# Router products turned before they are stored, the first segment's left q and k taken from SBUF, and one load and one store for each routed row

## The chip, the cores and the metric

The kernel runs on one core of a Trainium2 chip. The metric is the device time of one execution in microseconds (us); less is better. Engines are called as in the profile: PE (TensorE, matmuls and transposes), DVE (VectorE), ACT (ScalarE), POOL (GpSimd) and SP (SyncE). DMAs are issued from two queues here: SP's and POOL's. The core's 16 DMA engines work on both.

## What is computed

The output is `x + A(xn) + B(xn)`, where `xn` is the layer norm of `x` (2048 rows of 1024).

```python
def _A_ref(x, mem0, Wq, Wk, Wv, Wo, seg_len):      # H = 32 heads of 128, M = 8, seg_len = 32
    ...
    for s in range(n_seg):                          # 64 segments
        xs = x[:, s * seg_len:(s + 1) * seg_len, :].copy()
        h = jnp.concatenate([mem, xs], axis=1)      # 8 memory rows and 32 rows of x
        q, k, v = ...                               # h @ Wq, Wk, Wv
        scores = jnp.where(mask, q k^T * scale, -1e9)
        o = softmax(scores) v @ Wo
        mem = o[:, :M, :].copy()                    # memory for the next segment
        outs.append(o[:, M:, :])
    return jnp.concatenate(outs, axis=1)

def _B_ref(x, w_r, w_gate, w_up, w_down):
    r = x @ w_r                                     # one number for each row: the router
    idx = jnp.argsort(-r, axis=-1)[:, :2]           # the two best rows
    ...
    y = silu(x_sel @ w_gate) * (x_sel @ w_up) @ w_down
    y = y * sigmoid(r_sel)                          # added to these two rows of the output
```

## The kernel before, in words

**Segments.** A is sequential: a segment needs the memory of the one before. Of its 32 rows, 24 are computed in the chain together with the 8 memory rows of the carry (the main rows, 32 columns of a stationary operand). The last 8 rows of each segment are called left rows. They are not needed for their own memory, so those of four segments (32 rows) go through the weights together, in the shadow of the main rows. Their q and k are put to DRAM (`ql_d`) and fetched by the segment that needs them; their v stays in SBUF.

**Weights.** Wq, Wk, Wv and Wo are 64 granules of 512 KB. 43 stay in SBUF (`wres`); 21 are streamed through five slots (`g`) in every segment, one of them being kept in PSUM instead, and a quarter of another. In the first segment all granules come from the inputs, and POOL copies the streamed ones to DRAM scratch (`wsc`, line 337), from which later segments read them (line 313). A segment runs six phases of eight granules (q and k of heads 0 to 15, q and k of heads 16 to 31, v of both halves, lines 600 to 643), then the output projection WO over the 16 granules of Wo (lines 646 to 690).

**The order of work** is written out by hand. Each engine and each DMA queue works off its instructions in program order. `hooks[p, kc]` holds what PE and the others do after granule kc of phase p: the turn of a phase's q or k (line 481) at granule 3 of the next phase, scores of half 0 at (2, 6) and of half 1 at (4, 6), the softmax at (3, 0) and (5, 0). `after(s, g)` (line 411) runs behind granule g: in the first segment it also issues the router's steps (`side`), block copies, x loads and resident loads, and `fetch()` issues the next streamed granule, which must wait on SP for a free slot.

**Around the change.** While a phase has left rows, `behind` (line 608) holds their passes and `after` back until the fourth granule. The router: line statistics of all rows, then 16 calls of `router_tile` (line 209, two DVE passes over 128 x 1024 each) behind granules 18 to 33; `router_out` (line 216) behind granule 34; `router_top` (line 220) behind granule 42, which reads the 2048 products back as one row (RROW) and finds the two best with MAX8 and FIND_INDEX8. The scratch for this lies in places of resident granules that come late: XR and RROW in the place of granule 61, MISC (RF, RB) in that of 63, the x rows XP in those of 49 to 60, XP7 (the last router tiles) in that of 49. So a Wo granule can be loaded only when the tile in its place has been read (lines 420 and 421).

The first segment's left q and k go the same way as the others': evacuated as XBl (line 633), stored to `ql_d` by four DMAs (line 636), and, since no later segment fetches them, loaded again by `scores` (line 499) itself: `new_lx(0, half)` clears a tile and loads four strips of 16 rows, `turn_lx` turns it into QKL, and `left_keys` copies the left k beside the main k.

**The end.** Lines 729 to 797: the two routed rows of x are loaded, normalised and turned; two rows of the output are loaded as four halves (ROW, line 767); the gate and up weights (GU), then the down weights (YP) are multiplied; YP is copied out of PSUM (line 792), scaled and added to ROW (line 794), and stored as four halves (line 797). T0 holds x of the two rows first and the copied YP later. Source and target rows are chosen by values that POOL reads from the index tile.

Of the kernel before, what the change touches and what calls it, by code (L numbers as in the profile page):

```python
# [8 lines left out]
BF16 = mybir.dt.bfloat16  # L9
F32 = mybir.dt.float32  # L10
U32 = mybir.dt.uint32
ALU = mybir.AluOpType
# [15 lines left out]
def kernel(  # L28
# [16 lines left out]
    nc = tc.nc  # L45
    P = 128
# [8 lines left out]
    NT = S // P  # L55
# [5 lines left out]
    XL = M  # L61
# [3 lines left out]
    out2 = out[0]  # L65
# [26 lines left out]
    one = ctx.enter_context(tc.tile_pool(name="one", bufs=1, reuse_waits="tile"))  # L92
    rot = ctx.enter_context(tc.tile_pool(name="rot", bufs=3, reuse_waits="tile"))
# [10 lines left out]
    r_d = dram.tile([1, S], BF16, name="r_d")  # L104
# [3 lines left out]
    def home(g, shape, dtype, name):  # L108
        return wres.tile(shape, dtype, name=name, tag=f"wres{g}")
# [105 lines left out]

    def router_out():
        nc.vector.tensor_copy(out=RB, in_=RF)
        nc.gpsimd.dma_start(out=r_d[0].rearrange("(t p) -> p t", p=P), in_=RB)

    def router_top():  # L220
        RROW = home(hx, [1, S], BF16, "RROW")
# [207 lines left out]

    n_x_left = list(range(n_x, NT // 2))  # L430

    def new_lx(s, half=None):

        t = lx[0] = one.tile([P, 512], BF16, tag="pt", name="LX") if half is None else \
            rot.tile([P, 512], BF16, tag="xb", name="LX")
        G, j = divmod(s, 4)
        if half is None:
            nc.gpsimd.dma_start(out=t[:, :], in_=ql_d[G][j])
        else:
            nc.vector.memset(t[:, :], 0.0)  # L440
            for jq in range(4):
                nc.gpsimd.dma_start(out=t[32 * jq + 16 * half:32 * jq + 16 * half + 16, :],
                                    in_=ql_d[G][j, 32 * jq + 16 * half:32 * jq + 16 * half + 16, :])

    lx = [None]

    def turn_lx():
        PTq = PTB.rearrange("p (i c) -> p i c", i=4)
        for il in range(4):
            nc.tensor.transpose(out=PTq[:, il, :], in_=lx[0][:, il * P:(il + 1) * P], identity=IDENT[:, :])  # L450
        t = qkl[0] = one.tile([P, 16, 4, XL], BF16, tag="qkl", name="QKL")
        nc.scalar.copy(out=t.rearrange("p h c r -> p (h c r)"), in_=PTq.rearrange("p i c -> p (i c)"))  # L452

    qkl = [None]
    todo = []
# [12 lines left out]
    for s in range(NSEG):  # L468
# [12 lines left out]
        def transposes(mat, half, XB):  # L481
            PTq = PTB.rearrange("p (i j r) -> p i j r", i=4, j=4)
            for il in range(4):
                nc.tensor.transpose(out=PTq[:, il, :, :].rearrange("p j r -> p (j r)"), in_=XB[:, il * P:(il + 1) * P],  # L484
                                    identity=IDENT[:, :])
            pv = PTq.rearrange("p i j r -> p (i j) r")
            if mat == 0:
                QT[half] = one.tile([P, 16, 32], BF16, tag="qt", name="QT")
                nc.scalar.copy(out=QT[half][:, :, :], in_=pv)
            else:  # L490
                KT[half] = one.tile([P, 16, NK], BF16, tag="kt", name="KT")
                if s > 0:
                    left_keys(half)
                nc.vector.tensor_copy(out=KT[half][:, :, 0:32], in_=pv)  # L494

        def left_keys(half):
            nc.vector.tensor_copy(out=KT[half][:, :, 32:NK], in_=qkl[0][:, :, 2 * half + 1, :])  # L497

        def scores(half):
            if s == 0:  # L500
                new_lx(0, half)
                turn_lx()
                left_keys(half)
            QKL = qkl[0]
            q, k = QT[half], KT[half]
            for il in range(4):
                for jq in range(4):
                    hh = 4 * il + jq
                    nc.tensor.matmul(SPS[32 * jq:32 * jq + 32, il, 0, :], lhsT=q[:, hh, :], rhs=k[:, hh, :],
                                     start=(il == 0), stop=True, tile_position=(0, 32 * jq), skip_group_check=True)  # L510
                    nc.tensor.matmul(SPS[32 * jq:32 * jq + XL, il, 1, :], lhsT=QKL[:, hh, 2 * half, :],  # L511
                                     rhs=k[:, hh, :], start=False, stop=True, tile_position=(0, 32 * jq),
                                     skip_group_check=True)
            S4 = SPS.rearrange("p i a k -> p i (a k)")
            nc.vector.tensor_tensor(out=S4, in0=S4, in1=MASK[:, :].unsqueeze(1).to_broadcast([P, 4, 2 * NK]), op=ALU.add)  # L515
            S8 = SPS.rearrange("p i a k -> p (i a) k")
            NM = one.tile([P, 8], F32, tag="nm", name="NM")
            nc.vector.tensor_reduce(out=NM[:, :], in_=S8, axis=AX.X, op=ALU.max, negate=True)
            nc.vector.tensor_tensor(out=S8, in0=S8, in1=NM[:, :].unsqueeze(2).to_broadcast([P, 8, NK]), op=ALU.add)
# [80 lines left out]
        for p, (mat, half) in enumerate(PHASES):  # L600
            PSm = psA.tile([P, 512], F32, tag="acc", name="PSm")
            PSl, done = None, []
            if mat in left:
                PSl, done = started.pop((s, p), (None, []))
                if PSl is None:
                    PSl = psL.tile([P, 512], F32, tag="accl", name="PSl")
            rest = [8 * p + kc for kc in range(KC) if 8 * p + kc not in done]
            behind = []
            for kc in range(KC):
                g = 8 * p + kc  # L610
                Gv = granule(g)
                for jq in range(4):
                    nc.tensor.matmul(PSm[32 * jq:32 * jq + 32, :], lhsT=ST[:, kc, :], rhs=Gv[:, 512 * jq:512 * (jq + 1)],  # L613
                                     start=(kc == 0), stop=(kc == KC - 1), tile_position=(0, 32 * jq))
                if g in kept_at and s == 0:
                    keep(g, Gv)
                behind.append((g, Gv))
                if PSl is None or kc >= 3 or not left_before:
                    for g_, Gv_ in behind:
                        if PSl is not None and g_ not in done:  # L620
                            left_pass(PSl, g_, Gv_, not done and g_ == rest[0], g_ == rest[-1])
                        after(s, g_)
                    behind = []
                for fn in hooks.pop((p, kc), []):
                    fn()
            left_before = PSl is not None
            if mat < 2:
                XB = rot.tile([P, 512], BF16, tag="xb", name="XB")
                nc.scalar.copy(out=XB[:, :], in_=PSm[:, :])  # L629
                hooks.setdefault((p + 1, 3), []).insert(0, lambda m=mat, h=half, b=XB: transposes(m, h, b))  # L630
                if PSl is not None:
                    XBl = rot.tile([P, 512], BF16, tag="xb", name="XBl")
                    nc.scalar.copy(out=XBl[:, :], in_=PSl[:, :])  # L633
                    c0 = 16 * half + 8 * mat
                    for jq in range(4):
                        nc.gpsimd.dma_start(out=ql_d[left[mat]][:, 32 * jq + c0:32 * jq + c0 + 8, :],  # L636
                                            in_=XBl[32 * jq:32 * jq + 32, :])
            else:
                c0 = half * 512
                VM[half] = rot.tile([P, 512], BF16, tag="xb", name="VM")  # L640
                nc.scalar.copy(out=VM[half][:, :], in_=PSm[:, :])  # L641
                if PSl is not None:
                    nc.scalar.copy(out=VL[:, c0:c0 + 512], in_=PSl[:, :])
# [117 lines left out]
    nc.tensor.matmul(PSG[0:2, 0:1], lhsT=SIGR, rhs=ONE1, start=True, stop=True)  # L761
    SIG = T2[0:2, 52:54].bitcast(F32)
    nc.vector.tensor_copy(out=SIG, in_=PSG[0:2, 0:1])
    ROW = rot.tile([2, 512], BF16, tag="xb", name="ROW0"), rot.tile([2, 512], BF16, tag="xb", name="ROW1")
    for c in range(2):
        for a in range(2):
            nc.gpsimd.dma_start(out=ROW[a][c:c + 1, :], in_=out2[bass.ds(vals[c], 1), 512 * a:512 * (a + 1)])

    GU = psA.tile([P, 512], F32, tag="acc", name="GU")
    for w in range(2):  # L770
# [12 lines left out]
    for fg in range(FC // 2):  # L783
        Gt = moe_tiles["dn", fg]
        for a in range(2):
            fc = 2 * fg + a
            for dh in range(2):
                nc.tensor.matmul(YP[dh][0:2, :], lhsT=HT[:, fc, :], rhs=Gt[:, a * D + dh * 512:a * D + (dh + 1) * 512],
                                 start=(fc == 0), stop=(fc == FC - 1))
    YB = T0[0:2, :]  # L790
    for dh in range(2):
        nc.vector.tensor_copy(out=YB[:, 512 * dh:512 * (dh + 1)], in_=YP[dh][0:2, :])
    for a in range(2):
        nc.vector.scalar_tensor_tensor(out=ROW[a][:, :], in0=YB[:, 512 * a:512 * (a + 1)], scalar=SIG[:, 0:1],
                                       in1=ROW[a][:, :], op0=ALU.mult, op1=ALU.add)
        for c in range(2):
            nc.gpsimd.dma_start(out=out2[bass.ds(vals[c], 1), 512 * a:512 * (a + 1)], in_=ROW[a][c:c + 1, :])


# [33 lines left out]
```

## Time and profile before

| what | value |
|---|---|
| three runs | 2170.11, 2173.65 (median), 2186.66 us |
| the profiled execution | 2172.97 us, of which the span of the page is 2171.4 us |
| PE, DVE, ACT, POOL busy | 78%, 36%, 31%, 30% of the span |
| DMA moved | 754.62 MB, mean 348 GB/s |
| first store of segment 0's output | 151.6 us |
| first store of the last segment's output | 2100.5 us |
| last output store issued | 2161.96 us |

Rows of a timeline read: start, duration, engine, line, operation, tiles out<-in, shape, count, and in brackets how long the engine was idle before and who ended that. A stretch (window) gives for each engine its busy time and instructions, then the clock granted to PE (1.00 is full), the mean busy share of the DMA engines, and what they moved. A tile's view ends with the least, median and largest time from issue to landing of its DMAs.

### The profile page before, as it was taken

The numbers are of one execution on the slowest core, as the hardware profiler recorded it, in microseconds if no ns is written. First come the engines' busy times: TensorE is split into PE (matmuls) and PEld (weight loads), VectorE is DVE, ScalarE is ACT, GpSimd is POOL, SyncE is SP. The second block draws the span as 40 slices with busy tenths as digits, with TensorE's granted clock in tenths as the row PEclk, the third lists the DMA queues.
The fourth block names the chain that finished last, engine by engine and source line by source line (L and its number), as shares of the span: only waits on it lengthen the run. The fifth ranks groups of instructions, "written<-read, shape, count | busy, mean of one in ns | idle before, by whom it ended". The sixth has DMA issues, their size and how long they took to land.

```text
span 2171.4 us, 82642 instructions
## 1 busy us (share of the span) xinstructions
PE 1683.9 (78%) x36007; PEld 904.3 (42%) x36007; DVE 781.9 (36%) x2463; ACT 671.1 (31%) x1865; POOL 643.6 (30%) x1218
## 2 busy tenths in 40 slices
PE   3247787878888887888888888878888788888754
PEld 1124444444444444445444444444444444444433
DVE  5613333332333333333333333333333333334320
ACT  0013233333333333333333333333333233333320
POOL 4223233332323233323323322332323233232120
PEclk8669999999999999999999999999999999999986
DMA  9989899998999999999999999999999999999996
GB/s 363 378 248 367 327 352 344 369 355 319 366 343 372 337 355 361 348 366 340 348 336 374 349 346 365 328 337 339 376 339 355 339 341 355 328 371 358 376 384 245
DMA packets 245244, 754.62 MB, mean 348 GB/s; under 512 B 49872, under 2 KB 56176, under 8 KB 244880
## 3 DMA queue, kind: packets, MB, share of 16 engines
q1 hardware_dynamic: 203440, 712.46, 88.0%
q0 software_dynamic: 41440, 36.86, 5.8%
q8 instruction: 282, 4.62, 0.9%
q14 instruction: 82, 0.67, 0.1%
HBM read 736.39 MB, written 22.95 MB: 350 GB/s over the span
## 4 chain that ended last, share of the span: by engine, by line
DMA 52%; PE 31%; issue 7%; ACT 4%; POOL 4%; DVE 2%; SPq 0%; ACTq 0%; DVEq 0%; POOLq 0%
DMA g<-wsc 34%; PE PSm L613 11%; DMA ql_d<-XBl 9%; PE WO L661 8%; DMA XL<-in_A_x_dram 3%; PE PSl L596 3%; PE WL L661 2%; POOL ql_d L636 2%; PE BO L549 2%; DMA LX<-ql_d 1%; POOL XL L272 1%; DMA XP<-in_A_x_dram 1%; ACT VM L641 1%; PE BT L251 1%; ACT XBl L633 1%
## 5 line engine op out<-in xcount | busy, mean ns | idle before, releaser
L613 PE MATMUL PSm<-wres,ST 128*32 128x512 bf16 x8192 | 702.1, 390 | 6.3 <-DVE ST L266 5.4
L613 PEld LDWEIGHTS <-ST 128*32 128x32 bf16 x12288 | 335.5, 96 | 598.4 <-issue 311.0
L613 PE MATMUL PSm<-g,ST 128*32 128x512 bf16 x4096 | 416.5, 390 | 204.0 <-DMA g<-wsc 186.2
L629 ACT CAST XB<-PSm 128x512 bf16<-128x512 f32 x256 | 150.2, 587 | 389.4 <-PE PSm L613 387.3
L636 POOL DMA_DIRECT2D ql_d<-XBl x256 | 152.9, 604 | 378.3 <-ACT XBl L633 364.5
L661 PE MATMUL WO<-wres,OT 128*32 128x256 bf16 x5632 | 254.8, 290 | 4.2 <-issue 4.1
L238 POOL DMA_DIRECT2D X<-in_A_x_dram x256 | 132.8, 526 | 366.8 <-PE WO L647 264.8
L706 POOL DMA_DIRECT2D out_dram<-OB x256 | 128.5, 509 | 378.5 <-DVE OB L704 373.0
L661 PEld LDWEIGHTS <-OT 128*32 128x32 bf16 x8192 | 207.9, 101 | 78.2 <-issue 44.0
L596 PE MATMUL PSl<-wres,STL 128*32 128x512 bf16 x2048 | 196.2, 394 | 1.1
L661 PE MATMUL WO<-g,OT 128*32 128x256 bf16 x2560 | 139.6, 294 | 26.3 <-DMA g<-wsc 15.2
L641 ACT CAST VM<-PSm 128x512 bf16<-128x512 f32 x128 | 76.9, 601 | 267.0 <-PE PSm L613 215.0
L556 DVE CAST OT<-BT 128x128 bf16<-128x128 f32 x128 | 37.3, 292 | 303.6 <-PE BT L551 303.6
L556 ACT CAST OT<-BO 128x128 bf16<-128x128 f32 x256 | 68.1, 266 | 220.4 <-PE BT L551 219.4
L549 PE MATMUL BO<-PT,VM 32*128 32x40 bf16 x1024 | 94.3, 180 | 45.6 <-ACT VM L641 42.1
L497 DVE COPY KT<-QKL 128x128 bf16<-128x128 bf16 x128 | 24.6, 192 | 266.2 <-ACT QKL L452 266.2
L549 PEld LDWEIGHTS <-VM 32*128 32x128 bf16 x2048 | 67.2, 92 | 122.0 <-issue 56.1
L515 DVE TENSOR_TENSOR BS<-BS,MASK 128x320 f32<-128x320 f32 x128 | 63.9, 500 | 134.9 <-PE BS L511 134.9
L596 PEld LDWEIGHTS <-STL 128*32 128x32 bf16 x3072 | 85.4, 99 | 57.9 <-issue 14.1
L494 DVE COPY KT<-BT 128x512 bf16<-128x512 bf16 x128 | 54.1, 422 | 148.4 <-PE BT L484 148.0
L246 POOL TENSOR_TENSOR X<-X,XN 128x256 bf16<-128x256 bf16 x64 | 42.8, 669 | 207.4 <-DVE XN L244 207.0
L596 PE MATMUL PSl<-g,STL 128*32 128x512 bf16 x1024 | 103.8, 389 | 0.1
(148 smaller groups left out, 2364.2 us busy)
## 6 DMA issues: line engine op xcount, KB each, us to landing
g<-wsc SPq DMA_DIRECT2D x1197, 512.0 KB, 6.3
g<-wsc SPq DMA_DIRECT2D x63, 384.0 KB, 4.7
ql_d<-XBl POOLq DMA_DIRECT2D x256, 32.0 KB, 5.9
LX<-ql_d POOLq DMA_DIRECT2D x63, 128.0 KB, 5.3
MW<-in_B_w_gate_dram SPq DMA_DIRECT2D x16, 448.0 KB, 9.4
MW<-in_B_w_up_dram SPq DMA_DIRECT2D x16, 448.0 KB, 9.3
wres<-in_A_Wk_dram SPq DMA_DIRECT2D x12, 512.0 KB, 12.3
wres<-in_A_Wo_dram SPq DMA_DIRECT2D x11, 512.0 KB, 6.9
```

Source lines behind the costliest of these rows:

```text
L238: nc.gpsimd.dma_start(out=X[s % 2][32 * g:32 * g + XM, :], in_=x2[s * SEG:s * SEG + XM, 256 * g:256 * (g + 1)])
L494: nc.vector.tensor_copy(out=KT[half][:, :, 0:32], in_=pv)
L515: nc.vector.tensor_tensor(out=S4, in0=S4, in1=MASK[:, :].unsqueeze(1).to_broadcast([P, 4, 2 * NK]), op=ALU.add)
L549: nc.tensor.matmul(o, lhsT=VM[half][q0:q0 + 32, il * P:(il + 1) * P], rhs=PTm[q0:q0 + 32, il, 0:NK], start=True, stop=False, tile_position ...
L556: copy(out=OT[half][:, 2 * ph + jl, :, :], in_=ov[:, :, 0:SEG])
L596: nc.tensor.matmul(PSl[32 * jq:32 * jq + 32, :], lhsT=STL[:, g % KC, :], rhs=Gv[:, 512 * jq:512 * (jq + 1)], start=first_, stop=last_, til ...
L613: nc.tensor.matmul(PSm[32 * jq:32 * jq + 32, :], lhsT=ST[:, kc, :], rhs=Gv[:, 512 * jq:512 * (jq + 1)], start=(kc == 0), stop=(kc == KC - ...
L629: nc.scalar.copy(out=XB[:, :], in_=PSm[:, :])
L636: nc.gpsimd.dma_start(out=ql_d[left[mat]][:, 32 * jq + c0:32 * jq + c0 + 8, :], in_=XBl[32 * jq:32 * jq + 32, :])
L641: nc.scalar.copy(out=VM[half][:, :], in_=PSm[:, :])
L661: nc.tensor.matmul(PS[32 * g:32 * g + 32, 0:256], lhsT=lhs(h), rhs=Gv[:, D * hs + 256 * g:D * hs + 256 * (g + 1)], start=False, stop=(last ...
L706: nc.gpsimd.dma_start(out=out2[s * SEG:s * SEG + XM, 256 * g:256 * (g + 1)], in_=OB[32 * g:32 * g + XM, :])
```

## The change

Three edits. `router_out` has PE turn the 128 x 16 products into 16 x 128, DVE copies them from PSUM to a new tile RT (in the place of granule 61), and the store writes 16 rows of 128 numbers. For the first segment the left q or k of a phase is turned from XBl directly, by four transposes and one ACT copy that takes the columns of segment 0 into QKL, just ahead of the turn of the same phase's main rows; so `scores` loads nothing, and the left k goes beside the main k where it does in other segments. XBl is still stored to `ql_d`. At the end ROW is one tile of two rows of 1024, in T0; each row is loaded by one DMA and stored by one, and the sum reads YP from PSUM.

```diff
     def router_out():
         nc.vector.tensor_copy(out=RB, in_=RF)
-        nc.gpsimd.dma_start(out=r_d[0].rearrange("(t p) -> p t", p=P), in_=RB)
+        nc.tensor.transpose(out=PTB[0:NT, 0:P], in_=RB, identity=IDENT[:, :])
+        RT = home(hx, [NT, P], BF16, "RT")
+        nc.vector.tensor_copy(out=RT[:, :], in_=PTB[0:NT, 0:P])
+        nc.gpsimd.dma_start(out=r_d[0].rearrange("(t p) -> t p", p=P), in_=RT[:, :])
...
-    def new_lx(s, half=None):
...
+    def new_lx(s):
+        t = lx[0] = one.tile([P, 512], BF16, tag="pt", name="LX")
         G, j = divmod(s, 4)
...
+        nc.gpsimd.dma_start(out=t[:, :], in_=ql_d[G][j])
...
+    def turn_first(mat, half, XBl):
+        if mat == 0 and half == 0:
+            qkl[0] = one.tile([P, 16, 4, XL], BF16, tag="qkl", name="QKL")
+        PTq = PTB.rearrange("p (i c) -> p i c", i=4)
+        for il in range(4):
+            nc.tensor.transpose(out=PTq[:, il, :], in_=XBl[:, il * P:(il + 1) * P], identity=IDENT[:, :])
+        nc.scalar.copy(out=qkl[0][:, :, 2 * half + mat, :], in_=PTB.rearrange("p (h s r) -> p h s r", s=4, r=XL)[:, :, 0, :])
...
                 KT[half] = one.tile([P, 16, NK], BF16, tag="kt", name="KT")
-                if s > 0:
-                    left_keys(half)
+                left_keys(half)
...
         def scores(half):
-            if s == 0:
-                new_lx(0, half)
-                turn_lx()
-                left_keys(half)
...
                     c0 = 16 * half + 8 * mat
+                    if s == 0:
+                        hooks[p + 1, 3].insert(0, lambda m=mat, h=half, b=XBl: turn_first(m, h, b))
...
-    ROW = rot.tile([2, 512], BF16, tag="xb", name="ROW0"), rot.tile([2, 512], BF16, tag="xb", name="ROW1")
+    ROW = T0[0:2, :]
     for c in range(2):
-        for a in range(2):
-            nc.gpsimd.dma_start(out=ROW[a][c:c + 1, :], in_=out2[bass.ds(vals[c], 1), 512 * a:512 * (a + 1)])
+        nc.gpsimd.dma_start(out=ROW[c:c + 1, :], in_=out2[bass.ds(vals[c], 1), :])
...
-    YB = T0[0:2, :]
     for dh in range(2):
-        nc.vector.tensor_copy(out=YB[:, 512 * dh:512 * (dh + 1)], in_=YP[dh][0:2, :])
-    for a in range(2):
-        nc.vector.scalar_tensor_tensor(out=ROW[a][:, :], in0=YB[:, 512 * a:512 * (a + 1)], scalar=SIG[:, 0:1],
-                                       in1=ROW[a][:, :], op0=ALU.mult, op1=ALU.add)
-        for c in range(2):
-            nc.gpsimd.dma_start(out=out2[bass.ds(vals[c], 1), 512 * a:512 * (a + 1)], in_=ROW[a][c:c + 1, :])
+        cols = slice(512 * dh, 512 * (dh + 1))
+        nc.vector.scalar_tensor_tensor(out=ROW[:, cols], in0=YP[dh][0:2, :], scalar=SIG[:, 0:1], in1=ROW[:, cols],
+                                       op0=ALU.mult, op1=ALU.add)
+    for c in range(2):
+        nc.gpsimd.dma_start(out=out2[bass.ds(vals[c], 1), :], in_=ROW[c:c + 1, :])
```

More of the change, by code (lines that the diff above doesn't have):

```diff
@@ L430 @@
     n_x_left = list(range(n_x, NT // 2))
-    def new_lx(s, half=None):
-        t = lx[0] = one.tile([P, 512], BF16, tag="pt", name="LX") if half is None else \
-            rot.tile([P, 512], BF16, tag="xb", name="LX")
+    def new_lx(s):
+        t = lx[0] = one.tile([P, 512], BF16, tag="pt", name="LX")
         G, j = divmod(s, 4)
[L437 to L443, printed above, removed]
+        nc.gpsimd.dma_start(out=t[:, :], in_=ql_d[G][j])
     lx = [None]
```

## The prediction

> **What bounds it now.** I read the page first, then stretches of the first 150 us and the timeline there engine by engine, then the last 20 us. All three edits lie in the first segment or behind the last one.
>
> ```profile
> span 2171.4 us, 82642 instructions
> GB/s 363 378 248 367 327 352 344 369 355 319 366 343 372 337 355 361 348 366 340 348 336 374 349 346 365 328 337 339 376 339 355 339 341 355 328 371 358 376 384 245
> DMA 52%; PE 31%; issue 7%; ACT 4%; POOL 4%; DVE 2%; SPq 0%; ACTq 0%; DVEq 0%; POOLq 0%
> ```
>
> Each number of the second line is a slice of 54 us. The third slice, 109 to 163 us, moves 248 GB/s, less than any but the last, in a kernel whose chain is half DMA. The stretches below cut it finer (columns: busy of PE, PEld, DVE, ACT, POOL, then granted clock, DMA share, GB/s).
>
> ```profile
> 60.00:98.00 38.00, 10.36 (x172) 4.88 (x172) 27.88 (x58) 5.02 (x8) 10.74 (x19) 0.65 1.03 403
> 98.00:106.00 8.00, 0.00 (x0) 0.00 (x0) 3.35 (x8) 0.00 (x0) 4.72 (x8) 0.50 0.87 295
> 106.00:124.00 18.00, 0.00 (x0) 0.00 (x0) 0.00 (x0) 0.00 (x0) 0.57 (x1) 0.50 1.01 100
> 124.00:134.00 10.00, 4.52 (x82) 2.49 (x86) 2.98 (x9) 2.08 (x4) 2.66 (x5) 0.55 1.00 371
> 134.00:142.00 8.00, 6.86 (x189) 4.10 (x182) 5.92 (x9) 3.51 (x16) 3.31 (x6) 1.00 0.77 243
> 142.00:148.00 6.00, 1.15 (x24) 0.97 (x24) 0.00 (x0) 0.00 (x0) 0.00 (x0) 0.60 1.03 384
> ```
>
> Up to 98 us the first segment runs at the DMA's rate, 403 GB/s: it brings in all weights, and copies the streamed ones for the later segments. Then come 18 us at 100 GB/s with the engines "busy" (share 1.01) and all of PE, DVE and ACT idle. What was issued there, and who waited:
>
> ```profile
> 101.16 1.19 POOL L218 DMA_DIRECT2D r_d<-MISC  x1 [3.50 <-DVE MISC L217]
> 123.43 0.69 POOL L337 DMA_DIRECT2D wsc<-in_A_Wo_dram  x1 [17.55 <-DMA r_d<-MISC]
> 125.03 0.50 POOL L222 DMA_DIRECT2D RROW<-r_d  x1 [0.92 <-DMA wsc<-in_A_Wv_dram]
> ...
> DMA to landing us min/median/max: 7.3/14.7/22.0
> ...
> 73.82 0.58 PE L450 MATMUL BT<-IDENT,LX 128*128 128x128 bf16 x4 [14.68 <-DMA LX<-ql_d]
> 128.58 0.59 PE L450 MATMUL BT<-IDENT,LX 128*128 128x128 bf16 x4 [43.35 <-DMA LX<-ql_d]
> 146.85 0.62 PE L661 MATMUL WO<-g,OT 128*32 128x256 bf16 x8 [5.64 <-DMA g<-in_A_Wo_dram]
> 149.55 0.62 PE L661 MATMUL WO<-g,OT 128*32 128x256 bf16 x8 [1.23 <-DMA g<-in_A_Wo_dram]
> ```
>
> The router products, 2048 numbers of 2 bytes with the partition as the fast index in DRAM, took 22.0 us to land (the larger landing of tile r_d), and every other transfer crept meanwhile. PE stood 43.35 us before the second half's left q and k (LX), because their load was queued behind that write. At the end PE waits for the last Wo granule. The other holds of the DMA are on SP's queue:
>
> ```profile
> 99.41 5.86 SPq L113 DMA_DIRECT2D wres<-in_A_Wo_dram  x7
> 133.56 0.37 SPq L311 DMA_DIRECT2D g<-in_A_Wo_dram  x1
> 133.97 5.60 SPq L113 DMA_DIRECT2D wres<-in_A_Wo_dram  x2
> ...
> 66.24 0.27 DVE L440 MEMSET LX<- 128x256 uint32 x1
> 75.84 0.50 DVE L515 TENSOR_TENSOR BS<-BS,MASK 128x320 f32<-128x320 f32 x1 [0.58 <-PE BS L511]
> 100.69 0.17 DVE L217 CAST MISC<-MISC 128x16 bf16<-128x16 f32 x1
> 134.55 2.24 DVE L223 MAX8 V<-RROW 1x8 f32<-1x2048 bf16 x1
> 136.91 2.27 DVE L224 FIND_INDEX8 I<-V,RROW 1x8 uint32<-1x2048 bf16 x1
> ```
>
> Seven Wo loads wait for the x rows whose places they take, that is for DVE's last router tile; the load at 133.56 waits for a stream slot, so for PE; one of the two at 133.97 takes the place of RROW and goes only when FIND_INDEX8 has read it (139.2).
>
> **Part 1 and 2, the first segment.** The bytes hardly change (two loads of 64 KB go). What counts is when the DMA has moved them. From 98 to 148 us it moved 8 x 295 + 18 x 100 + 10 x 371 + 8 x 243 + 6 x 384 = 12.12 thousand, so 12.12 MB. At the 403 GB/s of the 38 us before, that is 30.1 us: the last Wo granule comes 50 - 30.1 = 19.9 us earlier, if the queues never run dry. I check that they don't.
>
> DVE: the stall between the LX memset at 66.24 and the scores at 75.84 goes, for q and k of half 0 are then in SBUF. That is 9.6 us, so RB is done at 100.69 - 9.6 = 91.1. POOL's LX loads go too, and the copies behind them move up.
>
> PE now waits there. In the built order PE turns RB after granule 34's left pass, four granules before scores of half 1. Before, it went past this place; now it waits for DVE until 91.1, and behind it stand the left pass of granule 35, the new turn of half 1's left k, KT, and the scores. SP's loads that need slots wait with it. Counting a turn (0.6), an evacuation (0.3 to 0.6), KT (0.2 + 0.4) and three granules, scores of half 1 come about 5 us later, at 96, not 130. The new small operations, bounded by these rows:
>
> ```profile
> L556 ACT CAST OT<-BO 128x128 bf16<-128x128 f32 x256 | 68.1, 266 | 220.4 <-PE BT L551 219.4
> 34.54 0.42 DVE L324 COPY XK<-BT 128x512 bf16<-128x512 bf16 x1 [3.96 <-DMA ql_d<-XBl]
> L706 POOL DMA_DIRECT2D out_dram<-OB x256: 505/507/539, 151.6 to 2102.0; - x128
> ...
> DMA to landing us min/median/max: 1.8/4.1/6.5
> ```
>
> Each of the four new left turns is four transposes (0.6) and a copy of 128 x 128 (0.27), against two turns with a copy of 512 columns removed: 4 x 0.9 - 2 x 1.2 = 1.2 us more on PE's path. It costs nothing while PE waits for weights (10.36 us busy of 38); with that cover gone it costs 1.2. Holding XBl until its turn leaves one buffer of that tag for the four kept pieces; today the second of these waits 3.96 us for XBl's store, in the build it waits for the piece before it, about 1 us; nothing either way under the weights.
>
> The write of 16 rows has no row here. Below stands the store of OB rows (median 4.1 us to landing, most 6.5), above the write as it is (22.0). I take 6, nearer the store, whose rows of 512 bytes are the closest in form. Issued near 92, it lands at 98. Then RROW's load queues behind about four block copies: 0.52 MB each at half of 403 is 2.6 us, so RROW lands at 105 and FIND_INDEX8 is over 2.24 + 2.27 later, at 110. SP reaches the load for RROW's place after some ten others, of which the last two or three are still on their way: at 113 or so. There are 3 us to spare. The seven Wo loads go at 96 to 97, when the earlier ones have just landed or are landing; the copies fill the gap. So the DMA stays full, and I take 19.9 us. If RB stayed at 100.7, DMA would run dry from 97 for 4 us, and 15.9 remain. At 420 GB/s it would be 21.1.
>
> The Trainium skill (DMA: Bandwidth & Descriptors, section Where 436 GB/s comes from) gives about 358 GB/s as HBM's limit for a core. The trace does not agree over these 38 us, with 403. By its figure the sum would be 33.9 us for the same bytes, 16.1 gained, and a time of 2152.
>
> The later 63 segments repeat the same work with the same queues. They shift as a whole, so I take 0 for them, and the rivals price the rest.
>
> **Part 3, the end.**
>
> ```profile
> 2117.52 0.53 DVE L750 TENSOR_SCALAR T<-T,T 2x1024 bf16<-2x1024 bf16 x1
> 2151.39 2.75 PE L788 MATMUL YP<-g,T 128*2 128x512 bf16 x12
> 2153.97 1.28 DVE L792 CAST T<-YP 2x512 bf16<-2x512 f32 x2 [13.57 <-PE YP L788]
> 2155.17 1.39 DVE L794 SCALAR_TENSOR_TENSOR ROW<-T,T,ROW 2x512 bf16<-2x512 bf16 x2
> 2156.19 0.49 POOL L797 DMA_DIRECT2D out_dram<-ROW  x1 [42.26 <-DVE ROW L794]
> 2158.01 0.49 POOL L797 DMA_DIRECT2D out_dram<-ROW  x1 [1.33 <-DMA out_dram<-ROW]
> 2160.14 0.49 POOL L797 DMA_DIRECT2D out_dram<-ROW  x1 [1.65 <-DMA out_dram<-ROW]
> 2161.96 0.49 POOL L797 DMA_DIRECT2D out_dram<-ROW  x1 [1.33 <-DMA out_dram<-ROW]
> ```
>
> The stores wait for each other. After: no casts, so the two sums run from 2153.97 for 1.39 us (now out of PSUM; the casts that read it took 0.64 each, the sums 0.70, so I keep the price), to 2155.36. A store needs both halves now: issue 0.3 later at 2155.65, the second 1.82 after it at 2157.47 where the last was issued at 2161.96. That is 4.5 us; if a row of 2 KB took 0.4 longer, 4.1. The rows' load now waits until the normalisation has read T (2118.05) instead of going at 2111; it has 30 us before the sums and nothing stands behind it on POOL.
>
> **Sum.** 19.9 + 4.5 = 24.4 us off the profiled execution's 2172.97 is 2148.6. The median shown, 2173.65, is 0.7 above that execution, so I say 2149.
>
> **Rivals.**
>
> *Less of the DMA's time comes back.* The later segments move less than 403:
>
> ```profile
> 213.64:244.90 31.26, 24.63 (x582) 13.99 (x586) 11.62 (x39) 8.83 (x26) 7.79 (x15) 1.00 0.96 362
> 244.90:280.26 35.36, 27.92 (x575) 15.16 (x579) 11.25 (x37) 11.68 (x33) 10.24 (x20) 0.95 0.82 293
> ```
>
> At 362 GB/s the 12.12 MB take 33.5 us, 16.5 come back, and the time is 2152; with RB late as well, 2156. Against it: 403 held through PE's stalls and through copies. Chance 0.15, 2152 to 2158.
>
> *The edit does not free the DMA*: the slow 18 us come from writing the row to DRAM in small pieces as such, or from something else, and stay. Then 18 x (403 - 100) / 403 = 13.5 us of the 19.9 are not had: 6.4 + 4.5, 2162. For it: rows of 256 bytes are still short. Against it: 16 pieces stand for 2048, and OB's short rows land in 4.1 us. Chance 0.06. The Trainium skill (DMA: Bandwidth & Descriptors, section Specifications) says that transfers below 512 B are read, modified and written; 256 B fall under it, and no run here shows them alone.
>
> *Later segments give it back, and the kernel is slower.* Two segments stand above, from one first store of OB to the next: where PE's clock was halved for a while (mean 0.95), the segment took 35.36 us instead of 31.26. A first segment that ends elsewhere sets PE's pauses elsewhere in the others. At 4.1 us each, six more such segments of the 63 eat 24.4 us, and from there it is slower; twelve end at 2198. For it: runs of the same kernel lie from 2170.11 to 2186.66. Against it: nothing in the work of these segments changes. Chance 0.06 for 2160 or more, 0.02 of it slower by over 1%; as many fewer such segments give below 2141, chance 0.06. The Trainium skill (TensorE: Matmul & The Clock Gate, section on the HAM clock gate) has the array at half rate after an idle window of about 3.4 us; the trace agrees where PE idles, 0.50 from 106 to 124.
>
> **Numbers.** The forecast, 2141 to 2153, has 0.67. About 1%, 21.7 us, is what a measurement of this kernel can tell from no change, so faster by over 1% means below 2151.9: 0.64 of the forecast's 0.67 and the 0.06 below it, 0.70. Slower 0.02, same 0.28. The range 2139 to 2160 leaves out about 0.05 below and 0.12 above.
>
> **What would show it.** Right: r_d lands within 8 us; 98 to 128 us at 390 GB/s or more; no wait of PE for LX before the scores, one for RB near 91; the first store of OB near 132 instead of 151.6; two last stores, the last issued some 3.3 us after YP's matmuls end at 2154.14 in today's count. Wrong: a stretch under 300 GB/s that lasts, RB still at 100, SP's load into RROW's place going after 116, or the first store early and the 63 segments longer than (2102.0 - 151.6 - 1.5) / 63 = 30.9 us each (the last figure is the fourth store of its segment, 1.5 us behind the first).

## The result and the profile after

Five runs of the changed kernel have a median of 2156.0 us (2152.55 to 2157.31), five of the kernel before 2177.22 us (2170.11 to 2186.66). The ratio is 0.9896, with a 95% interval of 0.9864 to 0.9928: about 1.0% faster. Two later comparisons of the same pair gave 0.9854 (0.9799 to 0.9909) and 0.9861 (0.9816 to 0.9905). The forecast was 2149, 7 us too low; the range held the time.

The profiled execution took 2153.69 us, its span is 2152.1, 19.3 less than the 2171.4 of before. Three places make this sum: the first segment's output is stored 18.3 us earlier, the 63 later segments take 3.4 us more in all, and the end, from the last segment's first store on, is 4.4 us shorter. The first two are read from this row of tile OB (its first and last start; before, 151.6 to 2102.0):

```profile
L707 POOL DMA_DIRECT2D out_dram<-OB x256: 505/505/539, 133.3 to 2087.1; - x128
```

The stretches of the first segment after the change. The last two columns are DMA share and GB/s:

```profile
60.00:98.00 38.00, 18.50 (x253) 7.72 (x249) 32.07 (x68) 6.34 (x12) 12.22 (x22) 0.66 1.03 404
98.00:106.00 8.00, 4.47 (x85) 1.82 (x74) 1.93 (x6) 1.75 (x11) 1.81 (x4) 0.79 1.04 409
106.00:124.00 18.00, 5.29 (x92) 2.70 (x92) 5.41 (x7) 1.98 (x8) 2.90 (x6) 0.50 1.04 389
124.00:134.00 10.00, 4.92 (x70) 2.87 (x73) 0.89 (x4) 1.24 (x3) 0.69 (x2) 0.50 0.97 371
134.00:142.00 8.00, 7.87 (x116) 3.44 (x112) 0.88 (x3) 2.54 (x5) 3.21 (x7) 0.82 0.63 197
```

The 18 us at 100 GB/s are gone; the DMA runs at 371 to 409 until the segment's weights are in. The DMA share stood at 1.01 in the slow stretch too: the share does not tell a busy DMA from a useful one, only the GB/s does.

The router's row and what hangs on it, from the timeline of the changed kernel and the view of tile r_d:

```profile
90.67 0.17 DVE L217 CAST MISC<-MISC 128x16 bf16<-128x16 f32 x1
90.90 0.28 PE L218 MATMUL BT<-IDENT,MISC 128*16 128x128 bf16 x1 [5.96 <-DVE MISC L217]
91.79 0.52 POOL L221 DMA_DIRECT2D r_d<-RT  x1 [4.15 <-DVE RT L220]
96.81 0.50 POOL L225 DMA_DIRECT2D RROW<-r_d  x1 [2.25 <-DMA r_d<-RT]
106.13 2.28 DVE L226 MAX8 V<-RROW 1x8 f32<-1x2048 bf16 x1 [5.97 <-DMA RROW<-r_d]
108.52 2.27 DVE L227 FIND_INDEX8 I<-V,RROW 1x8 uint32<-1x2048 bf16 x1
131.28 0.62 PE L662 MATMUL WO<-g,OT 128*32 128x256 bf16 x8 [1.18 <-DMA g<-in_A_Wo_dram]
...
DMA to landing us min/median/max: 4.7/7.0/9.3
```

RB, the router products, comes 10.0 us earlier than before. PE now waits 5.96 us for it, as the order of the built program said. The DMA runs on at 404 and 409 GB/s in the stretches around that wait, and PE goes on to wait for weights anyway. The row lands in 4.7 us instead of 22.0, and is searched at 110.8. The load into its place was issued after 113, so the search held nothing. At 131.28 PE still waits for the last Wo granule: the DMA sets the end of the segment, as before.

The end, in the timeline of the changed kernel:

```profile
2137.54 2.75 PE L788 MATMUL YP<-g,T 128*2 128x512 bf16 x12
2140.11 1.40 DVE L792 SCALAR_TENSOR_TENSOR T<-YP,T,T 2x512 bf16<-2x512 f32 x2 [14.22 <-PE YP L788]
2141.80 0.48 POOL L795 DMA_DIRECT2D out_dram<-T  x1 [37.09 <-DVE T L792]
2143.66 0.48 POOL L795 DMA_DIRECT2D out_dram<-T  x1 [1.38 <-DMA out_dram<-T]
```

The two sums out of PSUM cost 1.40 us (1.39 before from SBUF), and the last store is issued 3.37 us after YP's last matmul (2140.29), where it was 7.82: 4.45 us sooner. That this is also the 4.4 us of the whole end is in part luck: the way from the last segment's first store to YP's last matmul took 54.7 us instead of 53.6, and the time from the last store to the end of the span 8.4 instead of 9.4.

### The profile page after: what moved, and what is told of

Same layout as the page of the kernel before. It is cut to its first block, busy times and chain, and to the rows that moved or that the text cites. A ratio compares the mean times of both kernels' runs of the same rounds, so it can differ in the third digit from the quotient of the medians.

```text
span 2152.1 us, 82631 instructions
## 1 busy us (share of the span) xinstructions
PE 1695.9 (79%) x36016; PEld 905.0 (42%) x36016; DVE 780.7 (36%) x2460; ACT 670.6 (31%) x1867; POOL 634.7 (29%) x1206
## 4 chain that ended last, share of the span: by engine, by line
DMA 51%; PE 32%; issue 6%; ACT 4%; POOL 4%; DVE 2%; SPq 0%; ACTq 0%; POOLq 0%; DVEq 0%
DMA g<-wsc 35%; PE PSm L612 12%; PE WO L662 8%; DMA ql_d<-XBl 8%; DMA XL<-in_A_x_dram 4%; PE PSl L595 3%; PE WL L662 3%; POOL ql_d L637 2%; PE BO L548 2%; POOL XL L275 1%; DMA XP<-in_A_x_dram 1%; PE BT L254 1%; ACT VM L642 1%; PE BT L488 1%; DVE XR L213 1%
## 5 line engine op out<-in xcount | busy, mean ns | idle before, releaser
L662 PE MATMUL WO<-wres,OT 128*32 128x256 bf16 x5632 | 254.2, 288 | 17.1 <-DMA wres<-in_A_Wo_dram 9.3
L595 PE MATMUL PSl<-wres,STL 128*32 128x512 bf16 x2048 | 201.0, 403 | 1.2
```

The costliest lines, as they stand in the source:

```text
L595: nc.tensor.matmul(PSl[32 * jq:32 * jq + 32, :], lhsT=STL[:, g % KC, :], rhs=Gv[:, 512 * jq:512 * (jq + 1)], start=first_, stop=last_, til ...
L662: nc.tensor.matmul(PS[32 * g:32 * g + 32, 0:256], lhsT=lhs(h), rhs=Gv[:, D * hs + 256 * g:D * hs + 256 * (g + 1)], start=False, stop=(last ...
```

## The experiments

Theory A: the first segment ends when the DMA has moved its bytes. The 2-byte store costs DMA time, and PE's waits for the left q and k (LX) cost almost none by themselves. Theory B: the waits of PE are what costs, and the slow stretch only lies beside them. The first store of OB is the measure; the profile gives it to 0.1 us. Without the 2-byte store it repeats: 133.3, 134.5 and 133.2 in three profiles of the changed kernel. With it, it does so less: 151.6 before and 156.5 in a second profile of the same first segment (the end alone, below).

**The router edit alone, the left q and k edit alone, the end alone** (each on the kernel before; the last two edits are shown in part)

```diff
# router edit alone
-        nc.gpsimd.dma_start(out=r_d[0].rearrange("(t p) -> p t", p=P), in_=RB)
+        nc.tensor.transpose(out=PTB[0:NT, 0:P], in_=RB, identity=IDENT[:, :])
+        RT = home(hx, [NT, P], BF16, "RT")
+        nc.vector.tensor_copy(out=RT[:, :], in_=PTB[0:NT, 0:P])
+        nc.gpsimd.dma_start(out=r_d[0].rearrange("(t p) -> t p", p=P), in_=RT[:, :])
```

> The kernel before with the router edit alone: the products are turned and stored as 16 rows; the first segment's left q and k still go through DRAM, the end is as before. Theory A (the first segment ends when the DMA has moved its bytes, and the 2-byte store costs DMA time): the first store of OB, 151.6 us before and 133.3 after, comes at 137 to 139, because DVE's stall before the first scores stays, RB is ready near 100.7, and the DMA runs dry for about 4 us. Theory B (what counts is PE's waits for the left q and k, 14.7 and 43.4 us, and the DMA's slow stretch only happens beside them): both waits stay, and the first store comes at 147 or later. The end of the kernel as before under both.

```diff
# left q and k alone: turn_first, and scores() without its load
+                    if s == 0:
+                        hooks[p + 1, 3].insert(0, lambda m=mat, h=half, b=XBl: turn_first(m, h, b))
...
-            if s == 0:
-                new_lx(0, half)
-                turn_lx()
-                left_keys(half)
```

> The kernel before with the left q and k of the first segment taken from SBUF, and nothing else: the products are still stored in pieces of 2 bytes. Theory A: the store still takes some 20 us to land and holds every other transfer for 18 us near 93 to 115, 13.5 us of DMA time are lost, and the first store of OB comes at 147 (145 to 150) in spite of PE never waiting for LX. Theory B: PE's waits are gone, and the first store comes at 133 to 136.

```diff
# the end alone
-    ROW = rot.tile([2, 512], BF16, tag="xb", name="ROW0"), rot.tile([2, 512], BF16, tag="xb", name="ROW1")
+    ROW = T0[0:2, :]
...
+    for c in range(2):
+        nc.gpsimd.dma_start(out=out2[bass.ds(vals[c], 1), :], in_=ROW[c:c + 1, :])
```

> The kernel before with the edit of the end alone (one load and one store for each routed row, the sum from PSUM). Both theories: the first store of OB stays at 151.6; from the last segment's first store of OB to the end of the span 66.5 us, where it was 70.9 before. If the chain of stores were hidden by something at the end of the program, 70 or more.

The router edit alone, first its stretches from 60 to 106 us, then PE's waits for LX and RB and the row of OB:

```profile
60.00:98.00 38.00, 9.39 (x144) 4.16 (x140) 27.94 (x58) 5.02 (x8) 10.71 (x19) 0.63 0.99 384
98.00:106.00 8.00, 3.55 (x33) 1.22 (x33) 3.83 (x9) 0.00 (x0) 3.96 (x8) 0.62 0.62 183
...
73.99 0.58 PE L453 MATMUL BT<-IDENT,LX 128*128 128x128 bf16 x4 [13.80 <-DMA LX<-ql_d]
101.08 0.27 PE L218 MATMUL BT<-IDENT,MISC 128*16 128x128 bf16 x1 [16.84 <-DVE MISC L217]
112.67 0.58 PE L453 MATMUL BT<-IDENT,LX 128*128 128x128 bf16 x4 [8.04 <-DMA LX<-ql_d]
...
L709 POOL DMA_DIRECT2D out_dram<-OB x256: 505/505/539, 139.8 to 2096.3; - x128
```

The left q and k alone:

```profile
98.00:106.00 8.00, 0.00 (x0) 0.00 (x0) 0.00 (x0) 0.00 (x0) 0.00 (x0) 0.58 1.02 41
...
110.39 0.62 PE L609 MATMUL PSm<-g,ST 128*32 128x512 bf16 x4 [15.30 <-DMA g<-in_A_Wv_dram]
...
DMA to landing us min/median/max: 9.0/14.8/20.6
...
L704 POOL DMA_DIRECT2D out_dram<-OB x256: 505/505/539, 147.9 to 2107.6; - x128
```

First store at 139.8 with the router edit alone (11.8 us of the 18.3), at 147.9 with the left edit alone (3.7 us earlier than in the profile of before, 8.6 earlier than in the second profile of the same first segment). B expected the reverse. The second run speaks against B: PE has no wait for LX, and the first store is still 14.6 us later than in the changed kernel. The wait has moved to a weight, 15.30 us, because the store still takes 20.6 us and DMA crawls at 41 GB/s. The first run does not part the theories as cleanly as was expected of it: PE waits 13.80 us for LX, nearly as before, but the second wait shrank from 43.35 to 8.04 us, since the load behind the store goes sooner, and 16.84 us for RB came instead.

With the left edit on top of the router edit, 6.5 us more come (139.8 to 133.3). The DMA's rates account for nearly all of it. The router edit alone makes PE wait for RB until 101, the loads behind that wait come late, and the DMA runs dry: 183 GB/s for 8 us, which is 8 x (403 - 183) / 403 = 4.4 us, and 384 instead of 404 in the 38 us before, another 1.9 us. A had 4 us for the dry stretch, and 137 to 139 for the store; it came 0.8 later.

The end alone: the last segment's first store was issued at 2110.2 and the span was 2175.5, so 65.3 us, 5.6 less than before (70.9); expected were 4.4 less. Its last two stores stand as in the changed kernel (the last 3.38 us behind YP's last matmul), which is 4.4 us. The rest is not the stores': 0.8 us less from the last segment's first store to YP's last matmul, and 0.3 less behind the last store. In the eleven profiles of this document the first of these lies between 52.8 and 56.1 us, with the same code but for the rows' load. Its first segment missed what was expected of it:

```profile
L706 POOL DMA_DIRECT2D out_dram<-OB x256: 505/505/539, 156.5 to 2111.7; - x128
...
DMA to landing us min/median/max: 7.5/16.7/25.9
```

The first segment is untouched there, but the store took 25.9 us to land instead of 22.0, and the first store of OB came 4.9 us later: the same code, and a cost that differs from run to run. So the first segment's gain lies between 17.1 and 23.3 us by these profiles, and the 18.3 of the first comparison is near the low end.

**A 2-byte store that nothing reads** (in the changed kernel)

```diff
         nc.vector.tensor_copy(out=RB, in_=RF)
+        nc.vector.tensor_copy(out=RB2[:, :], in_=RF)
...
         nc.gpsimd.dma_start(out=RROW[:, :], in_=r_d[:, :])
+        nc.gpsimd.dma_start(out=r_d2[0].rearrange("(t p) -> p t", p=P), in_=RB2[:, :])
```

> The changed kernel with one store added behind RROW's load on POOL: a copy of RB goes in 2-byte pieces to a DRAM tile that nothing reads. Theory A: nobody waits for it, yet the DMA crawls for 18 us, and the first store of OB comes 13.5 us later than in the changed kernel, at 147 (145 to 150). Theory B, or any in which only the waiting for the router's row costs: 133.3, within 1 us.

```profile
106.00:124.00 18.00, 0.00 (x0) 0.00 (x0) 4.63 (x3) 0.00 (x0) 1.58 (x3) 0.50 1.01 103
...
127.14 0.62 PE L666 MATMUL WO<-wres,OT 128*32 128x256 bf16 x8 [23.23 <-DMA wres<-in_A_Wo_dram]
...
95.87 29.06 SPq L114 DMA_DIRECT2D wres<-in_A_Wo_dram  x7
...
L711 POOL DMA_DIRECT2D out_dram<-OB x256: 505/505/539, 147.5 to 2110.9; - x128
```

The same seven loads in the changed kernel:

```profile
96.31 15.72 SPq L113 DMA_DIRECT2D wres<-in_A_Wo_dram  x7
```

The slow stretch is back, 103 GB/s over the same 18 us, and the first store is at 147.5, 14.2 us later (13.5 expected). PE does nothing in it. The store is on POOL's queue, and there only the LX load for the second segment waited for it (13.43 us), which the first segment does not read. SP's queue does not wait for the store, and yet its seven Wo loads take 29.06 us to go out instead of 15.72, and PE stands 23.23 us waiting for a Wo weight. B is out: the store costs through the DMA's rate, whoever waits.

**128 runs of 32 bytes instead of 16 of 256 or 2048 of 2**

```diff
-        nc.tensor.transpose(out=PTB[0:NT, 0:P], in_=RB, identity=IDENT[:, :])
-        RT = home(hx, [NT, P], BF16, "RT")
-        nc.vector.tensor_copy(out=RT[:, :], in_=PTB[0:NT, 0:P])
-        nc.gpsimd.dma_start(out=r_d[0].rearrange("(t p) -> t p", p=P), in_=RT[:, :])
+        nc.gpsimd.dma_start(out=r_d[0].rearrange("(p t) -> p t", p=P), in_=RB)
```

> The changed kernel without PE's turn of the products: RB is stored as it lies, 128 runs of 32 bytes (16 products of one partition), so the order of the row in DRAM is another; the index found at the end is not turned back, so other rows than the routed ones are patched. If the cost goes with the number of pieces: 22.0 us for 2048 pieces is 1.4 us for 128, r_d lands within 8 us, and the first store of OB stays at 133.3 within 1 us. If every piece under 512 bytes holds the DMA whatever their number, or the whole store is slow because of where it goes: r_d takes 15 us or more to land and the first store of OB comes at 145 or later.

```profile
DMA to landing us min/median/max: 6.1/7.2/8.3
...
L704 POOL DMA_DIRECT2D out_dram<-OB x256: 505/505/539, 133.8 to 2086.8; - x128
```

It lands in 6.1 us, the DMA moves 379 GB/s from 98 to 106 us and 391 from 106 to 124, and the first store is at 133.8. So being short is not enough: pieces of 32 bytes do not bring the slow stretch, and the rival that every piece under 512 bytes does is out. At 4 KB in all three, the number of pieces and their length change together, and in the 2-byte store neighbours in DRAM also come from different partitions. Which of these makes the cost no run here separates.

**Without the copies of Wq, Wk and Wv** (in the changed kernel)

```diff
-            nc.sync.dma_start(out=t[:, 0:n], in_=wsc[g][:, 0:n])
+            nc.sync.dma_start(out=t[:, 0:n], in_=(wsc[g] if g >= 48 else granule_dram(g))[:, 0:n])
...
-    to_copy = list(streamed)
+    to_copy = [g for g in streamed if g >= 48]
```

> The changed kernel without the copies of the 15 streamed granules of Wq, Wk and Wv to DRAM scratch: later segments stream them from the inputs themselves (rows of 4 KB either way); Wo's five are still copied. 7.7 MB fewer to move in the first segment. Theory A (DMA bytes set the first segment's end): 19 us less by bytes, but Wo's loads are issued only from 96 us on, when PE has passed the router's turn, so 14 granules of 1.3 us from there: first store of OB near 118 (115 to 121) instead of 133.3, and the time 12 to 16 us under the changed kernel, some 2141, if granules from the inputs stream as fast as copies. Rival (PE or DVE's chain sets the end): first store within 2 us of 133.3. Rival (inputs stream slower than copies): first store earlier, but the 63 later segments longer than 31.0 us each, and the time at or above the changed kernel's.

The kernel without these copies: a stretch before the late loads, one over the middle of the kernel, and the row of OB.

```profile
92.00:98.00 6.00, 4.04 (x37) 1.81 (x41) 2.31 (x7) 0.27 (x1) 0.53 (x1) 0.50 0.27 88
400.00:2000.00 1600.00, 1301.02 (x27732) 688.71 (x27732) 564.81 (x1821) 520.91 (x1460) 481.37 (x903) 0.96 0.95 341
...
L707 POOL DMA_DIRECT2D out_dram<-OB x256: 505/505/539, 123.9 to 2132.8; - x128
```

The changed kernel over the same middle:

```profile
400.00:2000.00 1600.00, 1317.09 (x28485) 706.20 (x28488) 573.47 (x1851) 533.09 (x1497) 489.60 (x919) 0.97 0.95 349
```

The first store comes 9.4 us earlier, so the copies do hold the first segment; 15 were expected, but the DMA ran dry before RB (88 GB/s from 92 to 98; RB was at 93.4) and stood at 268 GB/s from 98 to 106. And the later segments pay: the DMA moves 341 instead of 349 GB/s at the same share of 0.95, and a segment takes (2132.8 - 123.9 - 1.5) / 63 = 31.9 us instead of 31.0 or 31.1 in the three profiles of the changed kernel. The time is 2195.3 us, ratio to before 1.0038 (1.0005 to 1.0072); the changed kernel took 2155.44 beside it. The rival that inputs stream slower than copies holds. Why they do was not tested.

**Wo's copies in the second segment** (in the changed kernel)

```diff
-        if s == 0:
+        if s == 0 or (s == 1 and g >= 48):
             nc.sync.dma_start(out=granule_out(t, g), in_=granule_dram(g))
...
-    to_copy = list(streamed)
+    to_copy = [g for g in streamed if g < 48]
+    copy_later = [g for g in streamed if g >= 48]
...
+        if s == 1 and copy_later:
+            copy_block(copy_later.pop(0))
```

> The changed kernel with the five block copies of Wo's streamed granules moved from the first segment into the second, behind its first five granules, where the DMA of the changed kernel stands partly idle (134 to 142 us at 197 GB/s); the second segment reads these granules from the input. Theory A: 2.6 MB fewer before the first segment's end, 6.5 us: first store of OB at 126.8 instead of 133.3 or 134.5. In the second segment 6.5 us of DMA work fall on some 4 us of idle time, so its store, 31.1 us after the first in the changed kernel, comes 33 to 34 us after; 4 us net stay. Rival (the copies do not hold the first segment): 133 to 134.5. Rival (the copies hold the second segment as much as the first): nothing net. In the time, 4 us are less than the runs scatter.

```profile
126.71 2.00 POOL L710 DMA_DIRECT2D out_dram<-OB  x4 [18.93 <-DVE OB L708]
163.04 2.00 POOL L710 DMA_DIRECT2D out_dram<-OB  x4 [4.88 <-DVE OB L708]
```

The first store is where the bytes put it, 126.7 (126.8 expected). The second segment gives most of it back: its store comes 36.3 us behind, not 33 to 34. In the changed kernel the second store is at 164.4, 166.4 and 165.0 in three profiles, so 1.4 to 3.3 us are left of the 4 expected. The time, 2157.62 us, ratio 0.9891 (0.9850 to 0.9932), cannot be told from the changed kernel's. No version here beats it.

**The changed kernel again, twice**

> The changed kernel once more. The first segment should repeat: first store of OB at 133.3 within 1 us, RB near 90.7. The question is the later 63 segments, which took 31.0 us each in the first profile against 30.9 before (3.4 us in all): if that is chance of the PE clock's halved stretches, their sum differs here by several us either way; if it comes from the change, it is again some 3 us longer than before.

> The changed kernel for comparison on the same chip: first store of OB 133.3 to 134.5, the second segment's store some 31.1 us later, and the sum of the later 63 segments anywhere from 1950 to 1962 us, as in the profiles so far of both kernels (1949 to 1962).

The row of OB in the first of these profiles, and in the second:

```profile
L707 POOL DMA_DIRECT2D out_dram<-OB x256: 507/507/542, 134.5 to 2096.7; - x128
```

```profile
L707 POOL DMA_DIRECT2D out_dram<-OB x256: 505/507/539, 133.2 to 2096.5; - x128
```

Last less first, less 1.5 us for the fourth store, the 63 segments took 1952.3, 1960.7 and 1961.8 us in three profiles of one kernel. Before's 1948.9 is lower than all of them, and also than the 1953.7 of the run with the end edit alone, whose segments are before's own. So the 3.4 us of the first comparison lie well within what one kernel does from run to run; they are no cost that could be shown for the change, nor do two profiles with before's segments rule out one of a few us. The run times speak against it: the medians of the three comparisons lie 21.2, some 27 and some 28 us apart, and the first segment and the end account for 22.7 in the first.

## Why the prediction was right, and what was off

*The DMA's time sets the first segment.* Shown: a 2-byte store that nothing reads brings the first store of OB 14.2 us later, where 13.5 was worked out; without LX's waits but with that store it comes at 147.9; and 2.6 MB fewer to move bring it to 126.7, where 126.8 was worked out.

*19.9 us from the first segment.* 18.3 came. The bytes were right: by the first store of OB the DMA had moved 51.1 MB before (151.6 us at 337 GB/s) and 51.3 after (133.3 us at 385):

```profile
0.00:151.60 151.60, 47.91 (x727) 23.41 (x727) 74.73 (x187) 16.65 (x41) 45.19 (x98) 0.70 0.99 337
```

```profile
0.00:133.30 133.30, 58.98 (x736) 26.48 (x736) 74.37 (x186) 16.61 (x43) 40.53 (x89) 0.69 1.01 385
```

The term that was mis-sized is the rate: I took 403 GB/s for all of it, and the DMA did 409 up to 106 us but 389 up to 124 and 371 behind. 12.12 MB at these rates take 8 + 18 + 5 = 31 us against 30.1. The rest, 0.7 us, is not accounted for. And 18.3 is measured against one profile of before; against the second profile of the same first segment it would be 23.2, so that the term came out this close is in part luck. The limit of about 358 GB/s that the Trainium skill (DMA: Bandwidth & Descriptors, section Where 436 GB/s comes from) gives did not hold here: every stretch of the changed kernel from 60 to 134 us ran above it, at 371 to 409.

*DVE's 9.6 us, RB at 91.1, PE's new wait, the search over at 110, SP at RROW's place at 113.* Measured: RB at 90.7, scores of half 1 behind granule 38's passes at 95.6, RROW searched at 110.8, SP at its place at 113.6. The seven Wo loads began at 96.3 and took 15.72 us to go out, with the DMA full meanwhile. The 3 us to spare that I counted were there. RB late was priced at 4 us. With the router edit alone, where RB is still made only at 100.85, the first store came 6.5 us later than with both: 4.4 by the dry stretch, 1.9 by the slower one ahead of it.

*The write of 16 rows, taken as 6 us,* landed in 4.7. The rival that the edit would not free the DMA is out: 16 pieces of 256 B and 128 of 32 B landed in 4.7 and 6.1 us, and no slow stretch came. The rule of the Trainium skill beside it (DMA: Bandwidth & Descriptors, section Specifications: below 512 B read, modified, written) does not decide here, since both are below it.

*The end, 4.5 us.* The last store came 7.82 - 3.37 = 4.45 us sooner after YP, and about as much in every kernel with that edit. What lies ahead of YP scatters by more than 3 us.

*The later segments, taken as 0.* 3.4 of the 7 us by which the forecast of 2149 was too low lie here, and 1.6 in the first segment. Most of the other 2 is that the median of the five runs lies 2.3 us above the profiled execution, where I took 0.7. The sum was made on one execution of before whose later segments were the fastest of all the profiles here. The three profiles of the changed kernel spread over 9.5 us with nothing changed. The rival priced this at 4.1 us for each segment with a halved clock, from one extreme pair. The pair does not hold the same work either: 37 instructions of ACT and 26 of POOL in the longer stretch, 26 and 15 in the shorter. So the 4.1 us are not the clock's alone, and no run here tests that price.

## What to carry to other kernels

Where the DMA share is full and the GB/s are low, look for a transfer in many tiny pieces, also one that nobody waits for: it takes its time from every transfer beside it. Judge the removal of a wait by what is late next: the left q and k edit took 58 us of PE's waits for LX out of a stage and gave 3.7 us alone (8.6 against the second profile), because the DMA set the end; where the slow store was already gone it gave 6.5, because it kept the DMA from running dry. And work a change out on several profiles where stages scatter by more than the change is worth, those that it leaves alone among them.

## What the runs showed of the hardware

- A store of 4 KB in 2048 pieces of 2 bytes took 20.6, 22.0, 24.8 and 25.9 us to land in four profiles, and meanwhile all that the 16 DMA engines moved fell to 100, 103 or 66 GB/s over 18 us (41 GB/s over 8 us in the fourth), at a DMA share of 1.01 to 1.09. In 128 pieces of 32 bytes it took 6.1 us, in 16 of 256 bytes 4.7, and the DMA kept 391 and 389 GB/s from 106 to 124 us.
- With 15 of the streamed granules read from the inputs (rows of 4 KB at a pitch of 8 KB) the DMA moved 341 GB/s over 1600 us; with all of them read from copies laid end to end 348 or 349 in three profiles, at the same DMA share of 0.95.
